# A fused attention, expert and gated-convolution kernel: w1 in column quarters, and five pieces of work placed later

## The chip, the cores and the metric

The kernel runs on one core of one Trainium2 chip. Five engines each run their instructions in order: TensorE (PE, with its weight loads shown apart as PEld), VectorE (DVE), ScalarE (ACT), GpSimd (POOL) and SyncE (SP). Here SP only issues DMA transfers, and POOL issues some. The metric is the time of one execution in microseconds; smaller is better.

## The reference

Four batches of 576 positions with 8 heads of 64 go through three stages. The first is attention through 32 memory slots. The second sends each position to one expert, a two-layer network, with weight `p[e]`. The third is a gated convolution. In short:

```python
a = softmax(phi, over the sequence); k_m = a^T k; v_m = a^T v      # 32 slots a head
x = softmax(q k_m^T / 8) v_m                                       # 576 x 512 a batch
for s in positions:                                                # the expert of s
    fresh_e = argmax(logits[s])
    e = fresh_e if s == 0 or local_gate[s] < 0.5 else the expert of s - 1
    out[s] = p[s, e] * (relu(x[s] @ w1[e]) @ w2[e])                # 512 -> 1024 -> 512
h = relu(out @ w_in)                                               # 512 -> 1024
g = h * sigmoid(conv over s, 3 taps, of h)
result = g @ w_out                                                 # 1024 -> 512
```

## The kernel before

Every product is made of three matmuls of fp32r parts. `split` (L148, L149) makes the two parts of an operand: ACT copies it to a high part, DVE subtracts that from the source and leaves the low part. `matmul3` (L159) multiplies high by high, high by low and low by high.

**One batch in the expert stage.** The attention output is x = A V, where `att` holds A (128 rows of head and slot, two groups) and `vt` holds V. So x w1 = A (V w1), and the kernel multiplies V into w1 first. `vw_product` (L669) does that for one half of w1's columns out of two raw pieces `wa`, each of two heads and 512 columns: four small matmuls of 512 columns for each piece (L421; each stands twice in the trace, as 64x32 tiles of PE) into the PSUM tile `pv`, then the split to `vh` (ACT, L679) and `vl` (DVE, L681). Then come 8 products `h` (`hidden`, L684; `ph` in PSUM, six matmuls each; ACT L692 and DVE L693 leave the two parts of relu), and 4 products `y` (`second`, 24 matmuls each into `py`; ACT L757 copies to `ys`, POOL stores it, L758). That is done twice, for the two halves of the positions. So a batch has 24 steps, numbered 0 to 23: 8 h, 4 y, 8 h, 4 y. The four products of one bank size (`ph`, `py` and some small ones) share four PSUM banks, so a product can start only when the fourth before it has been read out. w2 arrives in four raw pieces `wb_jr`, and is split as `w2.b.j` into `wb`.

**What is put between these steps.** A table written by hand gives the order: `OPENING` (L40) up to the first y, `FIRST` (L52) for the second half of batch 0, and the dictionary in `order` (L83) for batches 1 to 3. An item at step i stands behind the h or y of that step. Items of the next batch's attention (`phi`, `psoft`, `pback`, `mem`, `back`, `scores`, `ssoft`, `asplit`), of routing (`frow`, `gatew`, `fcol`, `flog`, `rtok`, and at the end `rback`, `rall`, `rpp`, `rown`), and of the third stage are put there: `nar.i` turns a sixteenth of w_in and w_out from 64-bit words, loaded by `nload.i` into `nir`, into fp32 (two ACT instructions L221 and L222, DVE L223 to L226, a store by POOL), `win.k` splits the four pieces `wi` of w_in, and `ysplit.0` multiplies batch 0's y by p and splits it (L782, L149). `save.b` stores `att` and V to memory (L527).

**What sets the order on each engine.** PE runs in the order of the table. On the other engines a planner places instructions by estimated ready times, except those marked `keep_in_program_order` (ACT's part of `nar` for instance), which stay where the table has them, and those marked `urgent`. `issue_after` keeps an instruction from being placed ahead of a named one. SP loads raw pieces in the order of the queue `stages` into six buffers (`fetch`).

## Time and profile before

| | us |
|---|---|
| median of 3 runs | 441.5 |
| the runs | 441.5, 510.96, 441.15 |
| profiled execution | 439.97 |
| its span, first to last instruction | 438.0 |
| PE busy | 413.4 (94%) |
| DVE busy | 272.6 (62%) |
| ACT busy | 221.8 (51%) |
| POOL busy | 74.6 (17%) |
| PE's mean granted clock | 0.987 |

The profile gives each instruction's start and length on its engine. "Idle before" is the time for which the engine stood still ahead of an instruction, with the instruction or transfer that released it. The granted clock is 1 at 2.4 GHz and 0.5 at 1.2 GHz. The batches of the expert stage begin on PE at about 29, 79, 117 and 155 us in the order 0, 1, 2, 3 (batch 0's second half of h is at about 54 us), and the third stage's first product is at 232.04 us.

### The profile page before, as it was taken

To read this page: it belongs to the slowest core of one execution; us is meant where nothing else is said; L and a number is where in the kernel's file an instruction comes from. 1 tells how busy PE (TensorE), PEld (TensorE's weight loads), DVE (VectorE), ACT (ScalarE), POOL (GpSimd) and SP (SyncE) were. 2 spreads that over 40 slices of the span, in tenths; PEclk is the share of its full clock that TensorE was granted. 3 is DMA by queue.
4 is the path that set the end of the run, shared out by engine and by line. 5 is a ranking of instruction groups with operands and counts; after the bars stand their busy time and mean duration, and the time that the engine had idled before them with its cause. 6 is when DMAs were issued, how large, how long until landed. Compare 5 with 4: busy or idle time off the path is not lost.

```text
span 438.0 us, 7981 instructions
## 1 busy us (share of the span) xinstructions
PE 413.4 (94%) x3144; PEld 366.4 (84%) x3145; DVE 272.6 (62%) x482; ACT 221.8 (51%) x412; POOL 74.6 (17%) x123
## 2 busy tenths in 40 slices
PE   4789999889999999989899999999999999999994
PEld 3349968769998899789799998999889998899884
DVE  2468789469568877886773987078701885068600
ACT  4347467255556535666335882367512773267420
POOL 1000202001112021111010233014300143004300
PEclk9999999969999999999899999999999999999999
DMA  7899989943988079965540003200011000200012
GB/s 252 297 311 384 375 321 370 397 163 101 359 287 266 21 245 361 403 240 177 194 163 29 0 2 108 97 0 1 0 73 48 1 1 1 96 1 1 3 73 54
DMA packets 23245, 68.74 MB, mean 157 GB/s; under 512 B 3264, under 2 KB 3520, under 8 KB 23200
## 3 DMA queue, kind: packets, MB, share of 16 engines
q1 hardware_dynamic: 19616, 56.63, 37.4%
q0 software_dynamic: 3584, 11.54, 6.8%
q8 instruction: 26, 0.43, 0.4%
q14 instruction: 19, 0.16, 0.1%
HBM read 51.82 MB, written 16.33 MB: 156 GB/s over the span
## 4 chain that ended last, share of the span: by engine, by line
PE 79%; DMA 10%; DVE 6%; SPq 1%; ACT 1%; issue 1%; DVEq 0%; ACTq 0%
PE pi L159 23%; PE po L945 22%; PE py L159 18%; PE ph L159 9%; DMA kv<-in_kv 5%; DMA n4r<-in_w_in 3%; PE pk L399 2%; PE pv L421 2%; PE pl L540 1%; DMA y<-ydram 1%; DVE y L782 1%; DVE wi L149 1%; PE sc L421 1%; DMA p<-pdram 1%; DVE yl L149 1%
## 5 line engine op out<-in xcount | busy, mean ns | idle before, releaser
L159 PEld LDWEIGHTS py<-h,wb 128*128 128x128 f32 x768 | 102.9, 188 | 7.9 <-issue 6.2
L159 PE MATMUL py<-h,wb 128*128 128x288 f32 x768 | 108.6, 298 | 0.7 <-DVE h L693 0.7
L159 PE MATMUL pi<-yh,wi 128*128 128x288 f32 x512 | 90.4, 295 | 0.0
L945 PE MATMUL po<-wo,g 128*128 128x512 f32 (+1 forms) x408 | 90.2, 377 | 0.0
L945 PEld LDWEIGHTS po<-wo,g 128*128 128x128 f32 x408 | 72.8, 188 | 13.2
L159 PEld LDWEIGHTS pi<-yh,wi 128*128 128x128 f32 x512 | 76.3, 188 | 0.9
L927 DVE SCALAR_TENSOR_TENSOR ct<-ht,convw,ct 128x575 f32<-128x575 f32 x32 | 31.0, 968 | 56.7 <-ACT ct L926 56.7
L159 PE MATMUL ph<-att,vh 128*128 128x288 f32 x256 | 56.3, 313 | 5.9 <-ACT ys L757 3.4
L159 PE MATMUL pi<-yl,wi 128*128 128x288 f32 x256 | 54.6, 295 | 0.0
L159 PEld LDWEIGHTS ph<-att,vh 128*128 128x128 f32 x256 | 42.6, 197 | 12.1 <-ACT ys L757 3.6
L910 POOL CAST tail<-g 128x128 fp32r<-128x128 f32 x32 | 23.0, 719 | 125.3 <-DVE g L149 124.5
L159 PEld LDWEIGHTS pi<-yl,wi 128*128 128x128 f32 x256 | 41.1, 188 | 0.0
L159 PE MATMUL ph<-att,vl 128*128 128x288 f32 x128 | 39.2, 306 | 0.6 <-DVE vl L681 0.6
L924 ACT ACTIVATE ht<-pi 128x576 f32<-128x576 f32 x32 | 20.9, 653 | 36.1 <-PE pi L159 36.1
L692 ACT ACTIVATE h<-ph 128x288 fp32r<-128x288 f32 x64 | 25.5, 410 | 21.4 <-PE ph L159 21.2
L757 ACT ACTIVATE ys<-py 128x288 f32<-128x288 f32 x32 | 13.1, 410 | 44.8 <-PE py L159 28.4
L693 DVE SCALAR_TENSOR_TENSOR h<-ph,h 128x288 fp32r<-128x288 f32 x64 | 27.7, 448 | 12.1 <-ACT h L692 12.1
L758 POOL DMA_DIRECT2D ydram<-ys x32 | 17.3, 540 | 103.2 <-ACT ys L757 91.6
L905 DVE TENSOR_TENSOR ct<-ht,ct 128x576 f32<-128x576 f32 x32 | 27.8, 868 | 9.8 <-ACT ct L904 9.8
L969 ACT ACTIVATE ot<-po 128x512 f32<-128x512 f32 x17 | 9.5, 598 | 44.5 <-PE po L945 44.5
L148 ACT ACTIVATE g<-ct 128x576 fp32r<-128x576 f32 x32 | 21.8, 681 | 12.5 <-DVE ct L905 12.5
L929 DVE SCALAR_TENSOR_TENSOR ct<-ht,convw,ct 128x575 f32<-128x575 f32 x32 | 26.0, 812 | 0.3
(235 smaller groups left out, 505.5 us busy)
## 6 DMA issues: line engine op xcount, KB each, us to landing
kv<-in_kv SPq DMA_DIRECT2D x16, 512.0 KB, 10.8
q<-in_q SPq DMA_DIRECT2D x8, 576.0 KB, 11.3
ydram<-ys POOLq DMA_DIRECT2D x32, 144.0 KB, 4.7
y<-ydram SPq DMA_DIRECT2D x4, 1152.0 KB, 5.4
out<-ot SPq DMA_DIRECT2D x15, 256.0 KB, 2.0
ph<-in_phi SPq DMA_DIRECT2D x8, 288.0 KB, 8.7
adram<-at POOLq DMA_DIRECT2D x8, 288.0 KB, 7.0
wa_0r<-in_w SPq DMA_DIRECT2D x4, 512.0 KB, 3.7
```

The source lines that it names most:

```text
L148: pin(nc.scalar.activation(hi, src, AF.Copy))
L159: pin(nc.tensor.matmul(ps, st, mv[:, cols], start=i == 0, stop=i == len(terms) - 1))
L421: nc.tensor.matmul(ps[slots(h), g], left(g, h), right(g, h), start=True, stop=True)
L692: nc.scalar.activation(t[:, 0, :], ps, AF.Relu)
L693: low = nc.vector.scalar_tensor_tensor(t[:, 1, :], ps, 0.0, t[:, 0, :].bitcast(F32), ALU.max, ALU.subtract)
L758: nc.gpsimd.dma_start(ydram[b, d, :, half(hf)], yt)
L905: slow(f"gm.{f}").tensor_tensor(ct, ht, ct, ALU.mult)
L910: nc.gpsimd.tensor_copy(tail[:, f, :, to:to + 64], t[:, :, 512:576].bitcast(F32))
L924: nc.scalar.activation(two(ht), halves(ps), AF.Relu)
L927: nc.vector.scalar_tensor_tensor(ct[:, 1:], ht[:, :S - 1], convw[:, 0, f:f + 1], ct[:, 1:], ALU.mult, ALU.add)
L929: nc.vector.scalar_tensor_tensor(ct[:, :S - 1], ht[:, 1:], convw[:, 2, f:f + 1], ct[:, :S - 1], ALU.mult, ALU.add)
L945: nc.tensor.matmul(ps[:, cols], st[sp], w[:, mp, f % 2, cols], start=f == 0 and i == 0, stop=f == 7 and i == 2)
```

## The change

1. w1 is laid out so that each raw piece holds all four heads and 256 columns. `vw_product` multiplies a quarter of the columns out of one piece, by eight matmuls of 256 columns instead of four of 512. In batch 0 the four quarters stand one by one between the h products, and each is split on its own. In batches 1 to 3 two quarters follow each other and are split together, as one half was.
2. The fifth conversion (`nar.4`, `nload.6`) moves from step 22 of batch 0 to step 6 of batch 1, and those of batch 1 to 3 are placed anew. In batch 3, `nar.15` moves from step 1 to step 8.
3. In the second half of batch 0, `pback`, `mem`, `back` and `gatew` stand about a step later.
4. `w2.b.3` of batches 1 to 3 moves from step 3 to step 7. In batch 3, `rpp` (the transposes `pp`, L610) moves from step 7 to 8, `win.0` and `win.1` to step 10, `ysplit.0` from 16 to 19, `win.2` and `win.3` to 20 and, on ACT and DVE, into program order.
5. `save.b` is issued by POOL behind the latest store of a y, no longer behind the load of a piece of w2.
6. Batch 0's y times p is not placed ahead of the last low part of an h so far.

```diff
@@ -43,24 +43,23 @@
 pmax.2 pmax.3 frow.0 gatew.0 fexp.0 scores.0.0 strn.0.0 pexp.2 pexp.3 fcol.0 flog.0
 smx.0.0 ssub.0.0 scores.0.1 strn.0.1 sexp.0.0 pback.2 pback.3 ssum.0.0 ahi.0.0 prec.2 prec.3 alo.0.0 mem.2
 w1.0 kv.3 vw.0.0 wload.0.2 q.1.0 wload.0.3 q.1.1 nload.0 nload.1 phi.4 kv.4
-h.0 h.0 vw.0.1 h.0 h.0 w2.0.0 h.0 h.0 h.0 h.0 smx.0.1 w2.0.1 ssub.0.1 w2.0.2 sexp.0.1
+h.0 vw.0.1 h.0 vw.0.2 h.0 h.0 vw.0.3 h.0 h.0 w2.0.0 h.0 h.0 smx.0.1 w2.0.1 ssub.0.1 w2.0.2 sexp.0.1
 y.0 phi.5 kv.5 mem.3 ssum.0.1 w2.0.3 y.0 back.1 ahi.0.1 alo.0.1 nar.0 nload.2 y.0 gatew.1 frow.1 fexp.1 nar.1 nload.3 y.0
 fcol.1
 """.split()
 
 
 FIRST = {
-    12: "scores.1.0 flog.1 w1.1 psoft.4", 13: "ssoft.1.0 psoft.5 rtok.0", 14: "pback.4", 15: "pback.5",
-    16: "mem.4 scores.1.1 ssoft.1.1", 17: "mem.5 nar.2 nload.4", 18: "conv", 19: "back.2",
-    20: "asplit.1.0 asplit.1.1 gatew.2 nar.3 nload.5", 21: "vw.1.0 w2.1.0", 22: "vw.1.1 w2.1.1 nar.4 nload.6",
-    23: "w2.1.2 q.2.0 q.2.1 save.0",
+    12: "scores.1.0 flog.1 w1.1 psoft.4", 13: "ssoft.1.0 psoft.5 rtok.0", 15: "pback.4", 16: "pback.5 scores.1.1 ssoft.1.1",
+    17: "mem.4 nar.2 nload.4", 18: "mem.5 conv", 20: "back.2 asplit.1.0 asplit.1.1 nar.3 nload.5",
+    21: "gatew.2 vw.1.0 vw.1.1 w2.1.0", 22: "vw.1.2 vw.1.3 w2.1.1", 23: "w2.1.2 q.2.0 q.2.1 save.0",
 }
 
 
 def order():
 
 
-    words = [5]
+    words = [4]
 
     def each(c, *parts):
         return [f"{part}.{u}" for u in units(c) for part in parts] if c < B else []
@@ -85,7 +84,8 @@
             for i, more in {
                 1: of(c, "frow", "fexp") + [f"save.{b}"],
                 2: [f"rtok.{b}"] * whole + each(d, "phi", "kv"),
-                3: [f"scores.{c}.0", f"ssoft.{c}.0"] * whole + [f"w2.{b}.3"],
+                3: [f"scores.{c}.0", f"ssoft.{c}.0"] * whole,
+                7: [f"w2.{b}.3"],
                 8: of(c, "fcol") + [f"scores.{c}.1", f"ssoft.{c}.1"] * whole + each(d, "psoft"),
                 9: of(c, "flog", "w1"),
                 10: each(d, "pback"),
@@ -93,16 +93,16 @@
                 13: each(d, "mem"),
                 16: of(d, "back"),
                 18: of(d, "gatew"),
-                21: [f"vw.{c}.0", f"w2.{c}.0"] * whole,
-                22: [f"vw.{c}.1", f"w2.{c}.1"] * whole,
+                21: [f"vw.{c}.0", f"vw.{c}.1", f"w2.{c}.0"] * whole,
+                22: [f"vw.{c}.2", f"vw.{c}.3", f"w2.{c}.1"] * whole,
                 23: [f"w2.{c}.2"] * whole + [f"q.{d}.0", f"q.{d}.1"] * (d < B),
             }.items():
                 after[i] += more
-            for i in (5, 13, 15, 17, 19) if whole else (1, ):
+            for i in ((), (6, 13, 15, 17, 19), (4, 7, 13, 15, 17, 19), (8, ))[b]:
                 after[i] += narrow_next()
             if not whole:
-                for i, more in {0: "rtok.3 rback rall", 7: "rpp", 9: "rown", 10: "close yload.0",
-                                12: "win.0", 14: "win.1", 16: "ysplit.0", 17: "win.2", 20: "win.3"}.items():
+                for i, more in {0: "rtok.3 rback rall", 8: "rpp", 9: "rown", 10: "close yload.0 win.0 win.1",
+                                19: "ysplit.0", 20: "win.2 win.3"}.items():
                     after[i] += more.split()
         for i in range(0 if b else 12, 24):
             out += [f"h.{b}" if i % 12 < 8 else f"y.{b}"] + after[i]
@@ -284,11 +284,11 @@
 
             stage(name, F32, load, batch)
 
-        def w1_piece(name, pool, tag, bufs, eng=None):
+        def w1_piece(name, pool, tag, bufs, eng=None, pin=lambda ins: ins):
 
             raw = fetch(name)
             t = pool.tile([128, 2, 1024], F32R, tag=tag, bufs=bufs, name=name)
-            split(t[:, 0, :], t[:, 1, :], raw, eng)
+            split(t[:, 0, :], t[:, 1, :], raw, eng, pin)
             return t
 
         def w2_piece(name, eng=None, pin=lambda ins: ins):
@@ -526,7 +526,7 @@
 
         def save(b):
 
-            with behind(f"wb{max(b, 1)}_1"):
+            with tc.issue_after(stored[-1]):
                 for hf in range(2):
                     nc.gpsimd.dma_start(adram[b, hf], attf[b, hf].rearrange("p g t -> p (g t)"))
                 nc.gpsimd.dma_start(vdram[b], kvt[b][:, 1, :])
@@ -666,27 +666,34 @@
         ffn_cm = tc.tile_pool(name="ffn", bufs=1)
         fps = [ffn_cm.__enter__()]
 
-        def vw_product(vs, raws, c, name):
-
-            parts = [fps[-1].tile([128, 2, 512], F32R, tag="vw", bufs=4, name=f"{p}{name}_{c}") for p in ("vh", "vl")]
-            ps = banks(f"pv{name}_{c}")
-            by_head(ps, lambda g, h: vs[rows(g), slots(h)],
-                    lambda g, h: raws[h // 2][rows(g), h % 2 * 512:h % 2 * 512 + 512])
+        def vw_product(vs, raws, q, name, into=None):
+
+
+            hi, lo = into or (fps[-1].tile([128, 4, 2, 128], F32R, tag="vw", bufs=4, name=f"{p}{name}_{q // 2}")
+                              for p in ("vh", "vl"))
+            ps = banks(f"pv{name}_{q}")
+            at = q % 2
+            for i, raw in enumerate(raws):
+                cols = slice((at + i) * 256, (at + i) * 256 + 256)
+                by_head(ps[:, :, cols], lambda g, h: vs[rows(g), slots(h)],
+                        lambda g, h: raw[rows(g), h * 256:h * 256 + 256])
+            ps = ps.rearrange("p g (f n) -> p f g n", f=4)
+            first, last = 2 * at, 2 * (at + len(raws))
+            edges = (0, 1, 2) if name == "0" and q == 0 else (first, last)
             with urgent():
-                pieces = (slice(0, 128), slice(128, 512)) if name == "0" else (slice(0, 512),)
-                hi, lo = parts
-                for cols in pieces:
-                    nc.scalar.activation(hi[:, :, cols], ps[:, :, cols], AF.Copy)
-                for cols in pieces:
-                    nc.vector.tensor_tensor(lo[:, :, cols], ps[:, :, cols], hi[:, :, cols].bitcast(F32), ALU.subtract)
-            return parts
+                pieces = [slice(a, b) for a, b in zip(edges, edges[1:])]
+                for fs in pieces:
+                    nc.scalar.activation(hi[:, fs], ps[:, fs], AF.Copy)
+                for fs in pieces:
+                    nc.vector.tensor_tensor(lo[:, fs], ps[:, fs], hi[:, fs].bitcast(F32), ALU.subtract)
+            return hi, lo
 
         def hidden(vw, at, f, hf, name):
 
-            fs = slice(f % 4 * 128, f % 4 * 128 + 128)
             ps = bank(f"ph{name}_{hf}{f}")[:, :HALF]
+            hi, lo = vw[f // 4]
             matmul3([(ps, half(hf))],
-                    [((vw[f // 4][0][:, g, fs], vw[f // 4][1][:, g, fs]), (at[:, g, 0, :], at[:, g, 1, :])) for g in range(2)])
+                    [((hi[:, f % 4, g, :], lo[:, f % 4, g, :]), (at[:, g, 0, :], at[:, g, 1, :])) for g in range(2)])
             t = fps[-1].tile([128, 2, HALF], F32R, tag="h", bufs=8, name=f"h{name}_{hf}{f}")
             with urgent():
                 nc.scalar.activation(t[:, 0, :], ps, AF.Relu)
@@ -723,11 +730,21 @@
             pin = tc.keep_in_program_order if b == 0 or j == 3 else lambda ins: ins
             wbs[b, j] = w2_piece(f"wb{b}_{j}", slow(f"w2.{b}.{j}"), pin)
 
-        def expert_vw(b, c):
-            vws.setdefault(b, []).append(vw_product(kvt[b][:, 1, :], w1_half(f"{b}", c), c, f"{b}"))
-
-        def w1_half(name, c):
-            return [ahead.pop(f"wa{name}_{i}", None) or fetch(f"wa{name}_{i}") for i in (2 * c, 2 * c + 1)]
+        def expert_vw(b, q):
+
+            raw = ahead.pop(f"wa{b}_{q}", None) or fetch(f"wa{b}_{q}")
+            parts = vws.setdefault(b, [])
+            if b == 0:
+                part = vw_product(kvt[b][:, 1, :], [raw], q, f"{b}", parts.pop() if q % 2 else None)
+            else:
+                quarters.append(raw)
+                if q % 2 == 0:
+                    return
+                part = vw_product(kvt[b][:, 1, :], quarters, q - 1, f"{b}")
+                quarters.clear()
+            parts.append(part)
+
+        quarters = []
 
         ahead = {}
 
@@ -755,7 +772,9 @@
             yt = fps[-1].tile([128, HALF], F32, tag="ys", bufs=3, name=f"ys{b}{hf}{d}")
             with urgent():
                 nc.scalar.activation(yt, ps, AF.Copy)
-            nc.gpsimd.dma_start(ydram[b, d, :, half(hf)], yt)
+            stored.append(nc.gpsimd.dma_start(ydram[b, d, :, half(hf)], yt).ins)
+
+        stored = []
 
         def close():
             route_last()
@@ -779,7 +798,8 @@
             y, p = yp
             for d in range(4):
                 if p is not None:
-                    nc.vector.tensor_tensor(y[:, d, :], y[:, d, :], p, ALU.mult)
+                    with tc.issue_after(hidden_low[-1]) if b == 0 else contextlib.nullcontext():
+                        nc.vector.tensor_tensor(y[:, d, :], y[:, d, :], p, ALU.mult)
                 split(yh[:, d, :], yl[:, d, :], y[:, d, :])
 
         def y_parts(b):
@@ -795,7 +815,8 @@
             split_y(0, ys0[0], *ys0[1])
 
         def gated_w(kc):
-            wi[kc] = w1_piece(f"wi{kc}", late[1], "wi", 4, slow(f"win.{kc}"))
+            wi[kc] = w1_piece(f"wi{kc}", late[1], "wi", 4, slow(f"win.{kc}"),
+                              tc.keep_in_program_order if kc > 1 else lambda ins: ins)
 
         do = {
             "phi": load_phi, "kv": load_kv, "q": load_q,
@@ -867,7 +888,7 @@
                     nc.sync.dma_start(vx[:, 1, :], vdram[b])
                     for h in range(4):
                         stage_w1(lambda: src_w1(e), h, f"wa{nm}_{h}")
-                    xw = [vw_product(vx[:, 1, :], w1_half(nm, c), c, nm) for c in range(2)]
+                    xw = [vw_product(vx[:, 1, :], [fetch(f"wa{nm}_{q + i}") for i in range(2)], q, nm) for q in (0, 2)]
                     for j in range(4):
                         stage_w2(lambda: src_w2(e), j, f"wb{nm}_{j}")
                     xb = [w2_piece(f"wb{nm}_{j}") for j in range(4)]
@@ -1014,7 +1035,7 @@
 
         "phi": phi.reshape(U, 4, S, M).transpose(0, 1, 3, 2).reshape(U, 128, S),
 
-        "w1": moe_w1.reshape(E, 2, 2, 2, D, 2, 512).transpose(0, 5, 2, 1, 4, 3, 6).reshape(E, 4, 128, 1024),
+        "w1": moe_w1.reshape(E, 2, 4, D, 4, 256).transpose(0, 4, 1, 3, 2, 5).reshape(E, 4, 128, 1024),
 
         "w2": moe_w2.reshape(E, 8, 128, 4, 128).transpose(0, 3, 2, 1, 4).reshape(E, 4, 128, 1024),
         "w_in": moe2_w_in,
```

On PE in the opening (`pv` is V w1, `wa_0r` to `wa_3r` the raw pieces of w1, `ph` the h products), before:

```order
L421 MATMUL pv_0_395<-wa_0r,vt_240 32x512 x4
L421 MATMUL pv_0_395<-wa_1r,vt_240 32x512 x4
L159 MATMUL ph_00_426<-att_337,vh_0_393 128x288 x2
L159 MATMUL ph_00_426<-att_337,vl_0_394 128x288
...
L159 MATMUL ph_01_436<-att_337,vh_0_393 128x288 x2
L159 MATMUL ph_01_436<-att_337,vl_0_394 128x288
...
L421 MATMUL pv_1_448<-wa_2r,vt_240 32x512 x4
```

and now:

```order
L421 MATMUL pv_0_395<-wa_0r,vt_240 32x256 x8
L159 MATMUL ph_00_426<-att_337,vh_0_393 128x288 x2
L159 MATMUL ph_00_426<-att_337,vl_0_394 128x288
...
L421 MATMUL pv_1_436<-wa_1r,vt_240 32x256 x8
L159 MATMUL ph_01_447<-att_337,vh_0_393 128x288 x2
L159 MATMUL ph_01_447<-att_337,vl_0_394 128x288
...
L421 MATMUL pv_2_459<-wa_2r,vt_240 32x256 x8
```

The first h now stands behind one piece of w1 and no longer behind two, and a quarter stands ahead of the second h.

On ACT from the end of batch 0 to the first h of batch 1 (`ys012` and `ys013` are batch 0's last two y, `vh1_1` the second half of batch 1's V w1, `nd4` and `n4r` the fifth conversion, `wb1_2` the third piece of batch 1's w2), before:

```order
L757 ACTIVATE ys012_1124<-py01_2_1099 128x288
L679 ACTIVATE vh1_1_1127<-pv1_1_1129 128x1024
L221 ACTIVATE nd4_1143<-n4r_965 128x512
L222 ACTIVATE n4r_965<-n4r_965 128x512
L757 ACTIVATE ys013_1178<-py01_3_1153 128x288
L692 ACTIVATE h1_00_1198<-ph1_00_1191 128x288
L692 ACTIVATE h1_01_1208<-ph1_01_1201 128x288
L148 ACTIVATE wb1_2_1181<-wb1_2r_1092 128x1024
```

and now:

```order
L774 ACTIVATE ys012_1152<-py01_2_1127 128x288
L686 ACTIVATE vh1_1_1155<-pv1_2_1157 128x1024
L148 ACTIVATE wb1_2_1207<-wb1_2r_1120 128x1024
L774 ACTIVATE ys013_1204<-py01_3_1179 128x288
L699 ACTIVATE h1_00_1224<-ph1_00_1217 128x288
L699 ACTIVATE h1_01_1234<-ph1_01_1227 128x288
```

The conversion of `n4r` is gone from between `vh1_1` and `ys013`, and the copy of `wb1_2`, which stood behind two h, is there in its place.

On DVE in batch 3, around the second half's h products (`h_10` to `h_17` are their low parts, `wi` the pieces of w_in, `y` times `p` and `yl` the split of batch 0's y, then batch 1's y times p), before:

```order
L149 TENSOR_TENSOR wi_2754<-wi0r,wi_2754 128x1024
L782 TENSOR_TENSOR y_2712<-y_2712,p_2714 128x576 x2
L149 TENSOR_TENSOR wi_2777<-wi1r,wi_2777 128x1024
L782 TENSOR_TENSOR y_2712<-y_2712,p_2714 128x576 x2
...
L149 TENSOR_TENSOR wi_2824<-wi2r,wi_2824 128x1024
L149 TENSOR_TENSOR wi_2875<-wi3r,wi_2875 128x1024
L149 TENSOR_TENSOR yl_2801<-y_2712,yh_2800 128x576 x3
...
L693 SCALAR_TENSOR_TENSOR h_10_2751<-ph_10_2744,h_10_2751 128x288
...
L782 TENSOR_TENSOR y_2967<-y_2967,p_2969 128x576 x4
L693 SCALAR_TENSOR_TENSOR h_16_2834<-ph_16_2827,h_16_2834 128x288
```

and now:

```order
L149 TENSOR_TENSOR wi_2784<-wi0r,wi_2784 128x1024
L149 TENSOR_TENSOR wi_2787<-wi1r,wi_2787 128x1024
L700 SCALAR_TENSOR_TENSOR h_10_2825<-ph_10_2818,h_10_2825 128x288
...
L700 SCALAR_TENSOR_TENSOR h_17_2895<-ph_17_2888,h_17_2895 128x288
L802 TENSOR_TENSOR y_2780<-y_2780,p_2782 128x576 x4
L149 TENSOR_TENSOR yl_2899<-y_2780,yh_2898 128x576 x3
L802 TENSOR_TENSOR y_3035<-y_3035,p_3037 128x576 x4
L149 TENSOR_TENSOR wo_3153<-wo0r,wo_3153 128x1024
L149 TENSOR_TENSOR yl_2899<-y_2780,yh_2898 128x576
L149 TENSOR_TENSOR wi_2940<-wi2r,wi_2940 128x1024
L149 TENSOR_TENSOR wi_2943<-wi3r,wi_2943 128x1024
```

All eight low parts of h now stand ahead of y times p, of batch 0 and of batch 1, and of the last two pieces of w_in.

## Rows read from the trace of the kernel before

**Rows 1.** The page: busy time of each engine, its share, instructions.

```profile
PE 413.4 (94%) x3144; PEld 366.4 (84%) x3145; DVE 272.6 (62%) x482; ACT 221.8 (51%) x412; POOL 74.6 (17%) x123
```

**Rows 2.** Waits of PE: total us, times, longest.

```profile
PE ph L159 <- ACT ys L757: 3.4, 1, 3.4
PE ph L159 <- DVE h L693: 2.0, 1, 2.0
...
PE pp L610 <- DVE pack L602: 1.1, 1, 1.1
PE py L159 <- DVE h L693: 0.7, 1, 0.7
```

**Rows 3.** Windows: us, busy of PE, PEld, DVE, ACT, POOL; PEclk, DMA share, GB/s.

```profile
84.00:88.00 4.00, 1.94 (x15) 1.49 (x13) 0.00 (x0) 0.28 (x1) 0.00 (x0) 1.00 1.03 388
88.00:92.00 4.00, 2.71 (x12) 1.84 (x14) 3.52 (x9) 3.20 (x7) 0.70 (x2) 0.53 0.54 207
92.00:96.00 4.00, 4.00 (x31) 2.32 (x28) 1.86 (x5) 1.19 (x4) 0.38 (x1) 0.62 0.63 197
```

**Rows 4.** Timeline of ACT, 78 to 92 us: start, length, instruction [idle before <-releaser].

```profile
87.72 0.66 ACT L221 ACTIVATE nd<-n4r 128x512 f32<-128x512 f32 x1 [5.89 <-DMA n4r<-in_w_in]
...
88.84 0.40 ACT L757 ACTIVATE ys<-py 128x288 f32<-128x288 f32 x1
```

**Rows 5.** Timeline of SP, 58 to 92 us.

```profile
78.44 0.34 SPq L283 DMA_DIRECT2D wb_2r<-in_w  x1
```

**Rows 6.** DMA issues, 58 to 92 us: count, KB each, median us to landing.

```profile
adram<-at POOLq DMA_DIRECT2D x2, 288.0 KB, 7.4
...
wb_2r<-in_w SPq DMA_DIRECT2D x1, 512.0 KB, 10.5
```

**Rows 7.** Timeline of the opening, 24 to 40 us, all engines.

```profile
27.55 1.06 PE L421 MATMUL pv<-wa_1r,vt 64*32 64x512 f32 x8
...
28.68 1.09 ACT L679 ACTIVATE vh<-pv 128x256 fp32r<-128x256 f32 x2 [1.24 <-PE pv L421]
...
30.28 0.40 PE L159 MATMUL ph<-att,vl 128*128 128x288 f32 x1 [0.63 <-DVE vl L681]
...
31.87 0.63 PE L421 MATMUL pv<-wa_2r,vt 64*32 64x512 f32 x4
...
32.88 0.53 PE L159 MATMUL ph<-att,vh 128*128 128x288 f32 x2
...
33.39 0.42 PE L159 MATMUL ph<-att,vh 128*128 128x288 f32 x2
...
35.08 1.05 ACT L148 ACTIVATE wb<-wb_0r 128x1024 fp32r<-128x1024 f32 x1
...
36.17 1.22 DVE L149 TENSOR_TENSOR wb<-wb_0r,wb 128x1024 fp32r<-128x1024 f32 x1
```

**Rows 8.** Timeline of PE, 52 to 62 us: small matmuls of another size.

```profile
54.56 0.71 PE L421 MATMUL sc<-q,vt 64*32 64x288 f32 x16
```

**Rows 9.** Timeline of DVE, 198 to 236 us.

```profile
210.20 2.08 DVE L149 TENSOR_TENSOR yl<-y,yh 128x576 fp32r<-128x576 f32 x3
...
213.05 1.53 DVE L693 SCALAR_TENSOR_TENSOR h<-ph,h 128x288 fp32r<-128x288 f32 x4
...
218.53 2.76 DVE L782 TENSOR_TENSOR y<-y,p 128x576 f32<-128x576 f32 x4 [1.58 <-DMA y<-ydram]
```

**Rows 10.** Windows at the end of the experts, columns as in rows 3.

```profile
212.00:216.00 4.00, 2.46 (x13) 2.46 (x14) 3.10 (x10) 0.41 (x1) 0.00 (x0) 0.82 0.42 111
216.00:220.00 4.00, 4.00 (x26) 4.00 (x25) 1.93 (x4) 1.24 (x3) 0.00 (x0) 0.76 0.64 198
```

**Rows 11.** Timeline of PE, 190 to 236 us.

```profile
221.72 10.49 PE L159 MATMUL py<-h,wb 128*128 128x288 f32 x77 [0.69 <-DVE h L693]
232.04 0.43 PE L159 MATMUL pi<-yh,wi 128*128 128x288 f32 x2
```

**Rows 12.** The page: DMA issues over the whole span.

```profile
y<-ydram SPq DMA_DIRECT2D x4, 1152.0 KB, 5.4
```

## The prediction, made before the changed kernel was run

> **What bounds the kernel.** I read the busy times first [rows 1]. PE works 413.4 of the span's 438.0 us, so it is the bound, and only two things can shorten the run: fewer or faster PE instructions, or less of the some 25 us in which PE stands still. The change takes no arithmetic away. So I went to PE's waits, which name what ended each stop. Apart from the start and the end of the program, four of them are touched by the change [rows 2]: 3.4 us on ACT's `ys`, 2.0 us on DVE's low part of an h, 1.1 us on the routing's `pack`, and 0.7 us on another low part. For each I then read the timeline of the engine it waits for, to see what that engine was doing instead.
>
> The first stop is at the start of batch 1, where its fifth h needs a PSUM bank that `ys` must empty; it ends with that `ys` at 89.24 [rows 4], so it reaches from about 85.9. ACT stood for 5.89 us at the conversion of `n4r`, whose words had not landed, and the `ys` is behind it [rows 4]. The windows [rows 3] show two more things: DMA is full (share 1.03, 388 GB/s), and after the stop PE's granted clock is 0.53 for four microseconds and 0.62 for the next four, so it stood mostly at 1.2 GHz. With the work that PE did there, half speed cost about 2.71 x 0.5 + 4.0 x 0.38 = 2.9 us. The second stop is DVE's: the low parts of `h_10` to `h_13` start only at 213.05, behind a queue of conversions whose last long entry is `yl` [rows 9]; the first of the four is done at about 213.4, and PE stood from about 211.5. The clock behind it is 0.82 and 0.76 [rows 10], which costs about 2.46 x 0.18 + 4.0 x 0.24 = 1.4 us. The 0.7 us at 221.7 us [rows 11] is DVE again: `h_16` and `h_17` stand behind 2.76 us of batch 1's y times p, which had waited 1.58 us for its load [rows 9].
>
> **The fifth conversion, batch 0.** With `nar.4` gone from ACT, the wait on `n4r` and its two ACT instructions, of 0.66 us the one shown, go. But the order on ACT puts the copy of `wb1_2` in the same place, in front of the same `ys`, and that needs `wb_2r`. It was issued at 78.44 [rows 5] and took 10.5 us [rows 6]: it landed at 88.94. Its issue is held by the loads before it, so it comes earlier only as far as the full DMA has less to carry. The two stores of `att`, 2 x 288 KB or 0.59 MB [rows 6], leave the stretch, because `save.0` now stands behind batch 0's last y; at 388 GB/s [rows 3] that is 1.5 us. The burst itself begins with the opening's gain, 0.5 us (next part). So `wb_2r` lands near 86.9; a copy of 1024 columns takes 1.05 [rows 7], `ys` 0.40 [rows 4] and PE follows at about 88.4 instead of 89.3. **Gain 0.9 us.** The wait remains, with another name. I take the slow clock behind it as unchanged, since PE reaches the stop sooner, by the opening's gain and some tenths more, and stands about as long. DVE has the low part of `wb1_2` there in place of the conversion; that is 1.22 us [rows 7] against several instructions, so nothing new is late. The conversions of batches 1 to 3 lie where PE is never short of work; they cost nothing, and if that cover failed each would be worth at most its ACT time of 1.3 us. `pback`, `mem` and `gatew` are moved by a step ahead of the stop; whatever that gives is swallowed by the wait on `wb_2r`.
>
> **The quarters.** No row shows 32x256 products. Sixteen instructions of 512 columns take 1.01 us (from 31.87 to the next h at 32.88) [rows 7]; sixteen of 288 columns take 0.71 [rows 8]. A quarter is sixteen of 256 columns, so it lies between 0.51, half of the first, and 1.01, where the time goes by instructions and not by columns. I take 0.60, nearest to the row of 288 columns. In batch 0 four quarters cost 2.4 against 2.0 before. The first h no longer waits for the second piece (27.55, 1.06 us) and for half of the copy (of 1.09 us) behind it [rows 7]: it begins about 1.6 us sooner. Most of that is lost again, for the first y needs `wb_0`, and its copy and low part, 1.05 and 1.22 us [rows 7], end at 37.39 before and, now placed behind the sixth h, hardly sooner. I leave **0.5 us** for the opening, and it is already in the sum above, as the burst's earlier start. In batches 1 to 3 two neighbouring quarters do what two pieces did, in 1.0 to 1.2 us; at most 0.2 x 2 x 3 = 1.2 us more, which I put at 0.3 with the part in batch 3 that nothing hides. It stays inside the rounding of the sum and in the range.
>
> What the trace shows of switching between kinds of products: the h pair behind a `pv` takes 0.53 us, the next one 0.42 [rows 7], so about 0.1 us a change. The Trainium skill, "TensorEngine Tiling (Array Packing)", under Key Properties, says that changing the tiling mode drains TensorE, which speaks against quarters strewn between h products. Batch 0 has four such places for two; by the row that is 0.2 us more, and by the rule, if each drain also holds up the way in, the opening would give 0.1 instead of 0.5.
>
> **The end of the experts, batch 3.** Here all moves act on one queue, DVE's. Before `h_10` two low parts of `wi` remain, and they end long before PE gets there, so the 2.0 us of waiting goes. `y` times p is behind `h_17`, so the 0.7 us goes. `pp` is behind a y of 24 matmuls, which covers `pack`: the 1.1 us goes. With the stops goes the slow clock, 1.4 us. **Gain 2.0 + 0.7 + 1.1 + 1.4 = 5.2 us.** What is late next is what DVE now has left behind `h_17`: y times p 2.76, three `yl` 2.08, batch 1's y times p 2.76 [rows 9], `wo` 1.22, one `yl` 0.69 (a third of 2.08), and two `wi` of 1.22 [rows 7]: 11.95 us, and some 0.9 until `h_17` itself is done, 12.9. The cover is four y, 96 matmuls, at 10.49 / 77 us each [rows 11] 13.1 us, and the first `pi` needs the fourth piece of w_in only in its last quarter, over 2 us later. That fits with about 2 us to spare. The middle link, batch 1's y, has its load of 5.4 us [rows 12] start when `att` is free, at the end of `h_17`; DVE reaches it after 0.9 + 2.76 + 2.08 = 5.7 us, just in time.
>
> **The sum.** 0.9 + 5.2, less 0.3 for adjacent quarters, is 5.8 us. The profiled execution took 439.97 us, 2.0 more than its span, so 434.2 by it. The median of the runs is 1.5 us above that execution, which gives 435.7; the two lower runs differ by 0.35. I forecast **435.5 us**, and by itself this case reaches from 432 to 438: a quarter's price at its low end and an earlier burst on one side, a quarter of 0.71 us and a longer stop at `wb_2r` on the other.
>
> **The rivals.**
> *The wait at `wb_2r` vanishes.* PE would get to the bank at about 85, 0.5 and some tenths before 85.9. If `wb_2r` lands 3.3 us sooner still, at 83.6, copy and `ys` are done by then and the stop goes with its slow clock: 3.4 + 2.9 + 5.2 and the opening's 0.5, 12.0 us, or 429.5. For it: the load of `wb_2r` took 10.5 us for 512 KB in a full queue, so small changes ahead of it count. Against it: the stores are the only bytes that leave. Chance 0.14.
> *DVE late at `pi`.* If batch 1's y lands 2 to 4 us later than worked out, everything behind its product, the last two `wi` above all, is late, and PE stops once more at about 230 us, with the clock falling again: 2 to 3 us of the gain go back, 438. For it: 1.58 us were waited for just this load [rows 9]. Chance 0.12.
> *A quarter costs what a pair of pieces did* (the other side). At 1.01 us each, if the time goes by instructions, sixteen quarters cost 16 x 1.01 against 8 x 1.01 before, 8.1 us more, and with 5.2 + 0.9 gained the run is about 443.5, slower than before by 2 us. It is decided at 0.89 us a quarter, where gain and loss meet: 8 x (2 x 0.89 - 1.01) = 6.2, against 0.9 + 5.2. Against it stands the row of 288 columns with 0.71 [rows 8]; for it only that this row is more than 288/512 of the other. Chance 0.04. The same page of the Trainium skill, under Instruction Overhead, gives about 60 cycles for each matmul; by that a quarter would be an estimated (60 + 256) / (60 + 512) of 1.01, 0.56 us, and the sum better by 4 x 0.04 in batch 0.
> *That nothing changes*, because PE's order still has all of its waits, is excluded by the order on DVE, but for a general loss elsewhere I keep 0.03 at 441.
>
> **Chances and range.** My forecast has 0.67. The lower rival takes the range down to 429, and the DVE rival with a quarter of 0.71 us up to 439; what lies outside is about 0.15. Two per cent of 441.5 is 8.8 us, about what a measurement of this kernel can tell from no change, so "faster" means below 432.7: the lower rival with 0.14 and a seventh of the main case with 0.10 give 0.24. "Slower", above 450.3, is beyond every case worked out here; 0.03 for what I did not see. Within 2% is left with 0.73.
>
> **What would show it.** Right: PE's wait on `ys` stays, shorter than 3.4 us, and ACT's idle before it names `wb_2r`; the waits on DVE's h at 211 and 221 us and on `pack` are gone and the clock from 200 to 232 us is 1.0; a quarter's sixteen products take 0.55 to 0.7 us. Wrong: no stop near 85 us at all, a new wait of `pi` on DVE's `wi` or `yl`, or quarters near 1 us. A stop that I saw no reason for, between 95 and 190 us, where PE now never waits, would break the sum without touching its terms.

## The result and the profile after

The changed kernel takes 434.42 us (median of 4 runs, 433.77 to 434.75) against 441.32 us before (4 runs): a ratio of 0.9853, 95% interval 0.9824 to 0.9881, or 5.2 to 7.8 us less. Runs in a slower state (here one of 510.96 us, which the median before still contains) are left out of every ratio. The forecast was 435.5, within a range of 429 to 439. The profiled execution of after took 434.75 us, with a span of 433.0 against 438.0.

PE's part of the page's busy times, and PE's waits in the changed kernel (engine, line, releaser: us in total, times, longest), answer to [rows 1, 2]:

```profile
PE 410.8 (95%) x3272; PEld 366.5 (85%) x3273; DVE 275.8 (64%) x483; ACT 222.6 (51%) x413; POOL 74.5 (17%) x123
```
```profile
PE ph L159 <- ACT ys L774: 4.6, 1, 4.6
...
PE py L159 <- DVE wb L149: 0.7, 1, 0.7
```

Three of the four waits are gone: on `pack` and both on DVE's low part of an h. The fourth, on `ys`, has grown from 3.4 to 4.6 us, and a wait of 0.7 us in the opening is new. ACT's timeline (start, length, instruction, [idle before]) shows the cause of the growth, and the windows (us; busy PE, PEld, DVE, ACT, POOL; clock, DMA share, GB/s) what followed:

```profile
80.98 1.03 ACT L686 ACTIVATE vh<-pv 128x1024 fp32r<-128x1024 f32 x1 [0.68 <-PE pv L421]
89.34 1.06 ACT L148 ACTIVATE wb<-wb_2r 128x1024 fp32r<-128x1024 f32 x1 [7.33 <-DMA wb_2r<-in_w]
90.31 0.39 ACT L774 ACTIVATE ys<-py 128x288 f32<-128x288 f32 x1
```
```profile
84.00:88.00 4.00, 2.17 (x17) 1.71 (x15) 0.00 (x0) 0.00 (x0) 0.00 (x0) 1.00 1.02 398
88.00:92.00 4.00, 1.25 (x5) 1.25 (x6) 1.57 (x3) 1.96 (x4) 1.01 (x2) 0.61 0.30 120
92.00:96.00 4.00, 4.00 (x17) 2.10 (x15) 1.51 (x7) 1.31 (x4) 2.72 (x6) 0.54 0.90 322
```

As in [rows 3, 4] ACT stands for a load with `ys` behind it. It is now `wb_2r` in place of `n4r`, and it lands 1.6 us after the time at which the conversion of `n4r` began before (87.72). The clock falls as it did before.

At the end of the experts the windows answer to [rows 10], PE's timeline to [rows 11], and DVE's to [rows 9]. Between the windows stands one line of PE's timeline before, the last matmul of batch 3's first eight h, which the changed kernel's timeline begins with too:

```profile
212.00:216.00 4.00, 4.00 (x33) 4.00 (x32) 2.63 (x6) 1.65 (x4) 0.00 (x0) 1.00 0.28 74
216.00:220.00 4.00, 4.00 (x32) 4.00 (x32) 4.00 (x7) 3.56 (x6) 0.54 (x1) 1.00 0.93 320
```
```profile
192.83 0.30 PE L159 MATMUL ph<-att,vl 128*128 128x288 f32 x1
```
```profile
193.88 0.30 PE L159 MATMUL ph<-att,vl 128*128 128x288 f32 x1
...
214.38 12.86 PE L159 MATMUL py<-h,wb 128*128 128x288 f32 x96
227.08 0.43 PE L159 MATMUL pi<-yh,wi 128*128 128x288 f32 x2
```
```profile
215.40 2.75 DVE L802 TENSOR_TENSOR y<-y,p 128x576 f32<-128x576 f32 x4
218.07 2.09 DVE L149 TENSOR_TENSOR yl<-y,yh 128x576 fp32r<-128x576 f32 x3
220.32 2.76 DVE L802 TENSOR_TENSOR y<-y,p 128x576 f32<-128x576 f32 x4 [0.16 <-DMA y<-ydram]
...
225.94 1.22 DVE L149 TENSOR_TENSOR wi<-wi3r,wi 128x1024 fp32r<-128x1024 f32 x1
```

PE never stands here and its clock is 1.0. From the start of the last matmul of the first eight h to the first `pi` it takes 33.2 us (193.88 to 227.08); before, 39.2 (192.83 to 232.04 [rows 11]). That is 6.0 us gained here, and the 5.0 us by which the two spans differ are these 6.0 less the 1.05 us by which the changed kernel is late when it gets there. The queue behind `h_17` is the one that was worked out, link for link.

### The profile page after: what moved, and what is told of

It is laid out like the page before. It is cut to its first block, busy times and chain, and to the rows that moved or that the text cites. A ratio compares the mean times of both kernels' runs of the same rounds, so it can differ in the third digit from the quotient of the medians.

```text
span 433.0 us, 8229 instructions
## 1 busy us (share of the span) xinstructions
PE 410.8 (95%) x3272; PEld 366.5 (85%) x3273; DVE 275.8 (64%) x483; ACT 222.6 (51%) x413; POOL 74.5 (17%) x123
## 4 chain that ended last, share of the span: by engine, by line
PE 86%; DMA 9%; ACT 1%; DVE 1%; SPq 1%; issue 1%; ACTq 0%
PE pi L159 23%; PE po L966 23%; PE py L159 21%; PE ph L159 11%; DMA kv<-in_kv 5%; DMA wb_2r<-in_w 3%; PE pk L399 2%; PE pv L421 2%; PE pl L540 1%; DMA wa_1r<-in_w 1%; PE sc L421 1%; PE pa L385 1%; SPq L340 0%; PE pfb L509 0%; DVE wb L149 0%
## 5 line engine op out<-in xcount | busy, mean ns | idle before, releaser
L948 DVE SCALAR_TENSOR_TENSOR ct<-ht,convw,ct 128x575 f32<-128x575 f32 x32 | 30.9, 966 | 53.3 <-ACT ct L947 53.3
L159 PE MATMUL ph<-att,vh 128*128 128x288 f32 x256 | 54.9, 307 | 5.2 <-ACT ys L774 4.6
L159 PEld LDWEIGHTS ph<-att,vh 128*128 128x128 f32 x256 | 41.4, 192 | 11.3 <-ACT ys L774 4.9
L159 PE MATMUL ph<-att,vl 128*128 128x288 f32 x128 | 38.2, 299 | 0.2 <-DVE vl L688 0.2
L950 DVE SCALAR_TENSOR_TENSOR ct<-ht,convw,ct 128x575 f32<-128x575 f32 x32 | 28.3, 885 | 0.4
```

Of the source, the lines that this page charges most:

```text
L159: pin(nc.tensor.matmul(ps, st, mv[:, cols], start=i == 0, stop=i == len(terms) - 1))
L948: nc.vector.scalar_tensor_tensor(ct[:, 1:], ht[:, :S - 1], convw[:, 0, f:f + 1], ct[:, 1:], ALU.mult, ALU.add)
L950: nc.vector.scalar_tensor_tensor(ct[:, :S - 1], ht[:, 1:], convw[:, 2, f:f + 1], ct[:, :S - 1], ALU.mult, ALU.add)
```

## The experiments

All times are medians; ratios are to the kernel before, run beside them on the same chip. There are two theories. **A:** the gain is the end of the experts alone; at the stop on `ys` nothing was won, because the planner put a copy that waits for a load ahead of the copy that frees the bank, whichever load that is. **B:** the load's landing decides (its place in the queue, the bytes beside it), and quarters and late stores help it.

**The third piece's copy later.** The change, with the split of `wb1_2` three h later and (not shown) in program order on ACT and DVE:

```diff
-    23: "w2.1.2 q.2.0 q.2.1 save.0",
+    23: "q.2.0 q.2.1 save.0",
-                3: [f"scores.{c}.0", f"ssoft.{c}.0"] * whole,
+                3: [f"scores.{c}.0", f"ssoft.{c}.0"] * whole + ["w2.1.2"] * (b == 1),
```

> The change, with the copy of batch 1's third piece of w2 placed three h products later and in program order, so that ACT's copy of batch 0's last y no longer stands behind a load. Theory (the load of that piece is the whole of the stop of 4.6 us, and the slow clock behind it follows from the stop): the stop and about 2.3 us of slow clock (1.25 x 0.39 + 4.0 x 0.46 by the windows from 88 to 96 us) go, PE's wait on ys falls under 1 us, granted clock 1.0 from 84 to 100 us; 434.4 - 6.5 = about 428 us. Rival (another late load or DVE's low part of the same piece holds PE soon after): the wait has another name a few us later, the clock still falls, 432 to 434 us.

430.29 us, ratio 0.9767 (0.9739 to 0.9795). The stop and the slow clock are gone, as A has it, though the load itself lands hardly sooner (88.7 us, against 89.3 in the change); windows, and the new place at which PE waits:

```profile
84.00:88.00 4.00, 4.00 (x29) 2.74 (x27) 1.75 (x5) 1.64 (x4) 3.12 (x6) 1.00 1.03 397
88.00:92.00 4.00, 4.00 (x42) 3.37 (x41) 2.72 (x8) 2.13 (x6) 0.61 (x2) 1.00 1.03 409
92.00:96.00 4.00, 4.00 (x31) 3.83 (x29) 3.93 (x8) 3.68 (x7) 0.00 (x0) 1.00 0.14 56
96.00:100.00 4.00, 3.50 (x35) 2.73 (x35) 4.00 (x12) 2.54 (x6) 1.08 (x2) 1.00 0.67 219
100.00:104.00 4.00, 2.77 (x22) 2.33 (x21) 4.00 (x11) 1.10 (x2) 0.54 (x1) 1.00 0.17 58
```
```profile
103.37 3.21 PE L159 MATMUL py<-h,wb 128*128 128x288 f32 x22 [1.23 <-DVE wb L149]
```

The gain is 4.1 us of the 6.5 expected: DVE, which has no idle time from 92 on but 0.07 us, is late, and PE loses 0.50 us to an h and 1.23 to the low part of the same piece.

**Stores early, the copy held first.** The change with `save` behind the second piece of w2 again, and the last `ys` held behind the copy of `wb1_2` (for which `w2.1.2` stands at step 22 of the table, not 23).

> The change, with the stores of att and V issued behind the second piece of w2 again, as before the change, and the copy of the third piece held in front of the last y's copy, where the change has it. Theory (the 0.65 MB of stores share a full DMA with the load): the load lands 0.65 MB / 400 GB/s = 1.6 us later, PE's wait on ys grows from 4.6 to about 6.2, the time to 436 us. Rival (the load's time is set by its place in SP's queue, not by these bytes): wait and time as with the change, 4.6 us and 434.4 us.

432.11 us, ratio 0.9806 (0.9781 to 0.9831): neither expectation. It was not the test that it was meant to be: the hold let the first h of batch 1 go ahead of the waiting copy too.

```profile
84.48 0.41 ACT L699 ACTIVATE h<-ph 128x288 fp32r<-128x288 f32 x1 [3.09 <-PE ph L159]
88.98 1.06 ACT L148 ACTIVATE wb<-wb_2r 128x1024 fp32r<-128x1024 f32 x1 [4.09 <-DMA wb_2r<-in_w]
89.94 0.39 ACT L775 ACTIVATE ys<-py 128x288 f32<-128x288 f32 x1
```

One copy of an h ahead of the wait frees a bank, PE does another h and `pl`, a product of the routing, in the meantime, and its wait is 2.8 us and not 4.6.

**Stores early, the same order.** The run before this one, with the first h held behind `ys` as well, so that these copies stand on ACT in the change's order. Of the edit only the part on the stores is shown; the holds come on top of it:

```diff
-            with tc.issue_after(stored[-1]):
+            with behind(f"wb{max(b, 1)}_1"):
```

> The change, with the stores of att and V issued early, as before the change, and every other engine's order as the change has it (the copy of w2's third piece, then the last y's copy, then the first h). Theory (in the run with early stores and another order the gain came from the first h's copy being ahead of the waiting copy, and the stores themselves cost): the load lands 1.1 us later after the burst's begin (28.9 us with late stores, 30.0 with early ones, in six traces), the stop on ys is 5.5 us, 435.3 us. Rival (early stores cost nothing or help): 432 to 434.4 us.

434.42 us, ratio 0.9844 (0.982 to 0.9868), the change's own time. ACT, and two of PE's waits:

```profile
90.93 1.06 ACT L148 ACTIVATE wb<-wb_2r 128x1024 fp32r<-128x1024 f32 x1 [8.62 <-DMA wb_2r<-in_w]
91.89 0.39 ACT L777 ACTIVATE ys<-py 128x288 f32<-128x288 f32 x1
```
```profile
PE pl L540 <- ACT ys L777: 4.5, 1, 4.5
...
PE ph L159 <- DVE fw L489: 0.4, 1, 0.4
```

The load does land later: from the issue of `wa_0r` to the landing of `wb_2r` it is 30.4 us here (60.55 to 90.91), and 29.2 to 30.4 (mean 29.9) in all ten traces with early stores; in the three with late ones 28.6 to 29.1 (mean 28.8). So the stores are worth about 1.0 us of landing, where 1.5 was predicted. Yet the time does not show it: PE's wait is 4.5 us and begins one h later, at `pl`. The expected 0.9 us of loss did not come. This does not show that the stores cost nothing: the fifth h waits for DVE's `fw` here and not for `ys`, that is, it got another bank than in the change, and PE had one h more to do before it stood.

**Stores early, nothing held.** Only the diff above, on the change.

> The change, with the stores of att and V issued early, as before the change, and nothing held: the planner then puts the last y's copy and the first h ahead of the copy of w2's third piece. Theory (late stores cost their gain by leading the planner to put that copy first; the stores themselves move the load by 1.2 us only): PE's wait on ys goes, one on h's copies of 1 to 3 us is left, 430.5 to 432 us. Rival (only the load's landing counts): 434.4 us or more.

431.15 us, ratio 0.9795 (0.9766 to 0.9825). It has the same stores as the run before and another order, for the planner now puts `ys` and the first h ahead. It is faster by 3.3 us by the medians and by 2.2 by the ratios, whose intervals just touch (0.982 and 0.9825). ACT, and what is left of PE's wait:

```profile
83.38 0.41 ACT L774 ACTIVATE ys<-py 128x288 f32<-128x288 f32 x1 [2.34 <-PE py L159]
84.12 0.41 ACT L699 ACTIVATE h<-ph 128x288 fp32r<-128x288 f32 x1 [0.33 <-PE ph L159]
88.73 1.06 ACT L148 ACTIVATE wb<-wb_2r 128x1024 fp32r<-128x1024 f32 x1 [4.19 <-DMA wb_2r<-in_w]
```
```profile
PE ph L159 <- ACT gated_rows L542: 2.3, 1, 2.3
```

`gated_rows` is ACT's copy of `pl`, behind the copy that waits. In these two traces the load also lands 2.2 us apart (88.7 and 90.9), 1.3 of it because the burst began sooner here, so they alone do not part order from landing. The run with the third piece's copy later does: it kept the late stores and gained 4.1 us by order. Together they carry A: late stores did harm, not by their bytes but because the planner, with them, put the copy first.

**The end alone.** The kernel before with items 4 and 6 of the change and, of item 2, the move of `nar.15`.

> The kernel before, with the moves in batch 3 alone (last piece of w2, routing transposes, pieces of w_in, batch 0's y, the last conversion). Theory: PE's waits on pack and on DVE's h go, the clock stays at 1.0 from 193 us to the first pi, which brings 5.2 to 5.8 us: 435.5 to 436.1 us, and the stop of 3.4 us on ys stays with the wait for n4r. Rival (the end gives the 4 us of waits but the clock falls elsewhere): 437 to 438 us.

433.9 us, ratio 0.9825 (0.9784 to 0.9866). The span of the profiled execution is 432.2, 5.8 less than before; the stop on `ys` is there as in [rows 2]:

```profile
PE ph L160 <- ACT ys L758: 4.0, 1, 4.0
```

So this part alone gives all that the change gives; the rest of the change sums to nothing that the intervals can tell.

**Quarters alone.** The kernel before with item 1.

> The kernel before, with w1 in quarters alone. Theory (by the trace of the change: the first h is earlier, but the first y waits 0.73 us for the low part of w2's first piece, which now stands behind later instructions): the opening loses 0.5 to 1.1 us against before, and the stop on ys keeps its 3.4 us: 441.5 to 442.5 us. Rival (as predicted: the opening gains 0.5 us): 440.8 us. A quarter's sixteen products take 0.60 us either way.

441.44 us, ratio 0.9996 (0.9971 to 1.002): no difference that can be measured; theory and rival lie 0.7 to 1.7 us apart, so the time does not separate them. The trace does for the opening: PE's wait on `wb` is there, 0.7 us. Other waits moved too, though the edit is far from them: the one on DVE's h at the end of the experts is 3.6 us against 2.0 before.

**The first piece of w2 earlier.** The change, and:

```diff
-h.0 vw.0.1 h.0 vw.0.2 h.0 h.0 vw.0.3 h.0 h.0 w2.0.0 h.0 h.0
+h.0 vw.0.1 h.0 vw.0.2 h.0 h.0 w2.0.0 vw.0.3 h.0 h.0 h.0 h.0
```

> The change, with the split of batch 0's first piece of w2 one quarter earlier in the opening, ahead of the fourth quarter. Theory (the opening's loss is the first y's 0.73 us wait for that piece's low part): the wait goes, the burst of loads begins 0.7 us sooner and the stop on ys ends sooner with it: 433.7 us. Rival (the piece lands too late for that place, or the fourth quarter's own split is late instead): a wait of h on vl or vh of 0.3 to 0.8 us takes its place, 434.4 us.

434.58 us, ratio 0.9854 (0.9824 to 0.9884). The rival's wait came in its place:

```profile
PE ph L159 <- DVE vl L688: 0.9, 2, 0.7
```

**The fifth conversion alone.** The kernel before with `nar.4` and `nload.6` moved from step 22 of batch 0 to step 5 of batch 1, and batch 1's own first conversion from step 5 to 6.

> The kernel before, with the fifth conversion alone moved to batch 1. The planner then puts the copy of w2's third piece behind two h, not ahead of the last y's copy. Theory (a copy ahead of ys that waits for a load is what stops PE, whichever load it is): PE does four h more before it waits, the stop on ys goes, a shorter one of about 1.5 us on an h's copy is left, most of the 2.9 us of slow clock goes: 441.3 - 4 = 437 us. Rival (the stop only changes its name): 440.5 to 441.5 us.

437.49 us, ratio 0.9918 (0.9892 to 0.9945). As A has it: two h are copied ahead of the wait, and PE finds work until the load is there.

```profile
83.22 0.41 ACT L757 ACTIVATE ys<-py 128x288 f32<-128x288 f32 x1 [2.30 <-PE py L159]
83.96 0.41 ACT L692 ACTIVATE h<-ph 128x288 fp32r<-128x288 f32 x1 [0.33 <-PE ph L159]
84.74 0.41 ACT L692 ACTIVATE h<-ph 128x288 fp32r<-128x288 f32 x1 [0.38 <-PE ph L159]
87.95 1.06 ACT L148 ACTIVATE wb<-wb_2r 128x1024 fp32r<-128x1024 f32 x1 [2.79 <-DMA wb_2r<-in_w]
```

PE is busy for 3.91 us of the four from 88 to 92, at a clock of 1.00. Some 2 us of the gain go back at the end of the experts, where this kernel has the old order: PE's waits on DVE's h are 4.8 us there in all, against 2.7 before.

**The end and the fifth conversion.** Those two together, without quarters, late stores and the later memory steps.

> The kernel before, with the moves in batch 3 and the fifth conversion's move, without quarters, late stores and the rest. Theory (the two gains add, and the rest of the change is worth nothing or less): 433.9 - 4 = 430 us, below the change's 434.4. Rival (quarters and late stores are worth something that the stop hides): 433 us or more.

429.77 us, ratio 0.975 (0.9725 to 0.9775): the fastest kernel of this study, 4.7 us below the change (whose interval, 0.9824 to 0.9881, lies clear of it). The two gains add. Of the stop a wait of 0.3 us is left, on `gated_rows`.

**With the memory steps later.** The kernel above with item 3 of the change.

> The kernel before with the moves in batch 3, the fifth conversion's move and, new, the memory steps of batch 2 (pback, mem, back, gatew) a step later as in the change. Theory (PE's 0.8 us wait on ex at 60 us is shortened, and nothing swallows it now that the stop on ys is gone): 0.4 to 0.8 us below the run without that, 429.0 to 429.4 us. Rival (the later mem and vt start something else late, or the planner goes back to a load ahead of ys): 429.8 us or more.

429.88 us, ratio 0.976 (0.9733 to 0.9788): the rival. The wait on `ex` at 60 us goes, but PE, now sooner at the same load, waits 1.4 us there:

```profile
PE ph L160 <- ACT gated_rows L543: 1.4, 1, 1.4
```

**With quarters.** The kernel with end and fifth conversion, and item 1.

> The kernel before with the moves in batch 3, the fifth conversion's move and, new, w1 in quarters. Theory (the opening loses 0.5 us from the first pk to the second, by eleven traces, and the pair of quarters elsewhere costs nothing): 430.3 us, 0.5 above the run without quarters. Rival (quarters help once the stop is gone, as predicted by 0.5 us): 429.3 us.

433.09 us, ratio 0.9817 (0.9781 to 0.9853). Quarters lose 3.3 us here by the medians, more than either theory; the two intervals just miss each other (0.9775 and 0.9781). The planner puts only one h ahead of the waiting copy, and two waits of PE are added to the 0.7 us of the opening. Below them stand the eighth h on ACT and on DVE, and the window behind it:

```profile
PE py L160 <- DVE h L701: 1.5, 1, 1.5
PE ph L160 <- ACT gated_rows L543: 1.2, 1, 1.2
```
```profile
96.94 0.44 ACT L700 ACTIVATE h<-ph 128x288 fp32r<-128x288 f32 x1
```
```profile
99.03 0.45 DVE L701 SCALAR_TENSOR_TENSOR h<-ph,h 128x288 fp32r<-128x288 f32 x1
```
```profile
100.00:104.00 4.00, 4.00 (x34) 3.52 (x34) 4.00 (x11) 1.92 (x5) 0.54 (x1) 0.70 0.74 238
```

The loss is not the opening's. PE begins batch 1 only 0.3 us later than in the kernel without quarters (84.67 against 84.36). Then the eighth h is late: its copy stands on ACT behind two conversions and a step of the softmax and starts at 96.94 (95.33 without quarters), and its low part, behind more of that work on DVE, starts at 99.03 (96.87). PE waits 1.5 us for it, and the clock behind that is 0.70 and 0.87 for four microseconds each; without quarters it is 1.00 in this stretch. At the next `pk` PE is 3.7 us late (115.33 against 111.66), all that the two spans differ by (431.2 and 427.5). So in these two traces it is an order that costs here, too, and not the quarters' own time.

## Why the prediction was right, and where it was not

- **The end of the experts** was right in mechanism and near in size: 5.2 us forecast, 6.0 in the trace of the change and 6.0 in that of the end alone (193.12 to 226.31). The waits were the 3.8 us read from [rows 2]. The other 2.2 us are work that took longer, and the term that was too small is the slow clock, put at 1.4 us by [rows 10]: the eight h around the longest stop took 8.2 us without the wait (208.17 to 218.36) against 6.4 now (207.97 to 214.38), 1.8 more. The last 0.4 lie around the other two stops and were not taken apart. The DVE rival failed as argued: the load of batch 1's y held DVE for 0.16 us, and the last piece of w_in was done at 227.16, 0.08 us behind the start of the first `pi` (227.08), which by the prediction's working needs it only over 2 us later.
- **The fifth conversion** had the wrong sign: 0.9 us of gain forecast, and of the signs given for being right one failed, for the wait on `ys` is longer than 3.4 us and not shorter. Stop and slow clock together were 3.35 + 2.9 us before and 4.58 + 2.3 after (1.25 x 0.39 + 4.0 x 0.46), 0.6 us worse; from the first h of batch 1 to its first y PE took 0.9 us longer (84.11 to 99.95 against 83.89 to 98.81). PE itself was only 0.2 us late at batch 1's first h: the later memory steps take away its wait of 0.8 us on `ex` (the run with the memory steps later shows the same), and the stop swallowed that, as predicted. The step that failed is the landing of `wb_2r`, put at 86.9 and seen at 89.3. That `wb_2r` would be the next wait, ahead of the same `ys`, was right. Of the 2.4 us, some 0.8 are the stores (from the issue of `wa_0r` 29.8 us before and 29.1 after, 0.7 less and not 1.5). The rest, 1.65, is the start of the burst of loads, put 0.5 us earlier and found 1.15 later; before and after:

```profile
59.12 0.35 SPq L279 DMA_DIRECT2D wa_0r<-in_w  x1
```
```profile
60.27 0.35 SPq L279 DMA_DIRECT2D wa_0r<-in_w  x1
```

- **The opening** is the greater part of the burst's late start. Its loss has two parts. 0.6 us are there already at the first long run of `pk` (25.14 against 24.55), ahead of the first quarter. Its start lies between 23.5 and 25.3 us in the five kernels without quarters (mean 24.5) and between 23.7 and 25.8 in the eight with them (mean 25.1); the loads ahead of it are the same, so I take this part for chance, which one trace of each kernel does not prove. From there to the second run of `pk` the five kernels without quarters take 16.2 to 16.8 us (mean 16.5), the eight with quarters 16.7 to 17.6 (mean 17.1): quarters lose 0.6 us where 0.5 of gain was forecast. The first h is 1.1 us earlier against that start, but the split of `wb_0` ends 1.15 us later and not "hardly sooner": ACT runs in order, and the copies of the fourth quarter and of the sixth h are ahead of it. The start of `pk` before and after, and PE in the changed kernel:

```profile
24.55 2.30 PE L399 MATMUL pk<-kv,a 128*32 128x128 f32 x36
```
```profile
25.14 2.31 PE L399 MATMUL pk<-kv,a 128*32 128x128 f32 x36
...
30.08 0.66 PE L421 MATMUL pv<-wa_1r,vt 64*32 64x256 f32 x16
30.67 0.54 PE L159 MATMUL ph<-att,vh 128*128 128x288 f32 x2
31.04 0.29 PE L159 MATMUL ph<-att,vl 128*128 128x288 f32 x1
31.18 0.42 PE L159 MATMUL ph<-att,vh 128*128 128x288 f32 x2
...
39.18 3.08 PE L159 MATMUL py<-h,wb 128*128 128x288 f32 x21 [0.73 <-DVE wb L149]
```

- **A quarter's price** was right: 0.59 us (30.08 to 30.67) for the 0.60 taken, so the rival on the other side was out. A change between kinds of products costs 0.12 us (0.54 against 0.42), as in [rows 7]. The drain that the Trainium skill names in "TensorEngine Tiling (Array Packing)", Key Properties, is thus no more than this in the trace. The opening's loss of 0.6 us is put down to the wait on `wb`, 0.7 us; taken away by an earlier split, it came back as a wait on `vl`, so that the link is read from the trace and not shown by a gain.
- **The rival of the vanished wait** was near in its price and wrong in its condition. The stop as it was does go, and 3 to 4 us with it (430.3 and 431.2 us in two ways on the change, against 434.4; 429.8 in the kernel without quarters and late stores), not by an earlier load but by a copy or two ahead of the wait. I had seen the new order on ACT and priced the load; I did not price the order itself.
- That the total was near is in part luck, for two errors have opposite signs: 0.8 us too little at the end, 1.65 too much before it (0.6 forecast, 1.05 lost). By the two profiled executions 5.2 us came of the 5.8 forecast; the medians differ by 6.9, and by the ratio it is 6.5.

## What to carry to other kernels

When an instruction that waits for a load is taken out from ahead of a copy that frees a bank, look for what the planner puts in its place: the name of the load hardly matters, one or two cheap copies ahead of it are worth more than a microsecond of landing. A move that helps transfers can lose its gain through the planner, which then schedules the load's consumer sooner (that it does so because it sees the load earlier is my reading; no run shows its reasons); hold such a consumer behind the copies that the bound engine needs. Where several edits come together, run each alone: here two of them gave 10.7 us by the medians, and the rest took 4.7 of it back. Most of that goes to quarters (3.3 us, by the order that came with them); the memory steps cost nothing, and late stores were not run alone on that kernel.

## What was not expected of the hardware

Stores of 0.65 MB while the DMA engines were full moved a load behind them by 1.0 us (28.8 against 29.9 us, means over three and ten traces), less than their bytes at the 398 GB/s of the stretch (1.6 us). And the granted clock did not follow every stop: behind 2.3 us without PE work it was 0.57 in the next window (stores early, nothing held), behind 1.35 us it stayed at 1.00 (memory steps later); but behind 1.52 us it was 0.70 (with quarters), and behind 1.89 us, at 211.7 us of the run with the fifth conversion alone, it stayed at 1.00.
